# Routed two-layer mixture-of-experts kernel: guard terms moved into a table's margin, a minimum in place of masks, and a search's and a balancing's first products at other places of the order

## The chip, the cores and the metric

One core of one Trainium2 chip runs the program. The time is device microseconds for one execution, as a median over several; the profile comes from one execution of its own. TensorE (PE in the profile, PEld for its weight loads), VectorE (DVE), ScalarE (ACT), GpSimd (POOL) and SyncE (SP) each work through their own list of instructions in the order in which it was written, and wait for each other by semaphores.

## The reference

Attention over 4 x 8 heads of 576 positions gives 2304 tokens of 512 numbers. Two expert layers follow, each with 8 experts and two weight matrices per expert.

```python
# first layer: each token to one expert, in the order of the logits, 288 tokens per expert at most
cap = N // E
order = np.argsort(-flat)
for idx in order:
    tok, e = (int(idx) // E, int(idx) % E)
    if assigned[tok] >= 0 or counts[e] >= cap:
        continue
    assigned[tok] = e
    counts[e] += 1
# h = relu(x[mask] @ w1[e]); out[mask] = h @ w2[e]

# second layer: all tokens through all experts, weighted by a balanced table
P = np.exp(logits - logits.max())
for _ in range(8):
    P /= P.sum(1, keepdims=True) + 1e-09
    P /= P.sum(0, keepdims=True) + 1e-09
    P *= N / E
out += P[:, e:e + 1] * (np.maximum(x @ w1[e], 0.0) @ w2[e])
```

## The kernel before

The order of every engine's work is written by hand: `interleave` (L700) runs a main generator, whose `yield`s say how many nanoseconds of TensorE work were just issued, and a side generator, whose `yield`s say how much of that work shall go by before its next part is issued. A smaller number puts the side's next part earlier into every engine's list.

The program has these parts. The attention goes first. `stage1` then runs the first layer, expert by expert, with the routing beside it. One `Router.phase` (L530) finds one expert's tokens. It searches a threshold over the bits of the logits in six counts (`STEPS`): VectorE compares the 18 x 128 logits with up to 64 candidates into a grid of zeros and ones `G` (`above`, L504, in two halves of 9 columns); TensorE sums the grid with 18 products (L576, into the bank `r`); VectorE compares the sums with the places left (`ok`, L585); TensorE multiplies once more (L588); VectorE takes the maximum (`cur`, L590), from it the next candidates `x`, and the next `G`. After the last count the chosen tokens are marked in `ze`, TensorE adds them up by a matrix of ones and a triangular one, `tri` (L618, L619), and VectorE makes each token's place in its expert's list of it: a running sum `pos` (L621), masked by `zv` (chosen and not beyond 288, L624 and L625), and the two halves of `pos` added (`r`, L627). From the places come the lists by which GpSimd gathers tokens and weights. `books` (L653) then takes the used tokens out of the next phase: `mask` is lowered by 100 where a token is used.

While phase `ph + 1` is searched, TensorE works on expert `ph`: `moe1` (first layer) and then `m2_l1`, `m2_l2` (the second layer's first expert, on a piece of 256 tokens). In `l1` (L907) a step is three products; ScalarE copies the upper half of each of the 8 results of a piece out of the bank (L912), VectorE the lower half (L913). These halves live in tiles that the profile calls `w1h` and `w1l` (`xt` and `xg` in the last two pieces). Beside this, gathered weights of the next expert are split into halves piece by piece: ScalarE the upper (L847), VectorE the lower one (`w1l<-raw`, L838). The parts come to VectorE in the order in which they were issued.

After the eight phases, `last` (L1410) runs the second layer's first expert on the last two pieces, with `direct(1)`, which makes sums and halves of the next expert's weights (L1028 to L1048), and `sinkhorn` as the side. `sinkhorn` (L1289) takes the maximum of the table `P` (128 x 18 x 8) over each partition (L1302), has TensorE transpose it (L1305), takes the maximum of that and scales it (L1306, L1307), spreads it by a product (L1309), and after the exponential (L1311) does eight rounds: sum over each row's 8 numbers, guard 1e-9, reciprocal, product; then a column sum by TensorE (L1322) and VectorE (L1323), guard, reciprocal, product. What is left of it runs beside the first block of `stage2` (`s_l1`, L1176), in which TensorE waits for additions of VectorE (L1147). `stage2` is the long part: seven experts over three blocks each, with a seven-product scheme.

Of the kernel before, what the change touches and what calls it, by code (L numbers as in the profile page):

```python
# [11 lines left out]
F32 = mybir.dt.float32  # L12
# [9 lines left out]
CAP = N // E  # L22
# [357 lines left out]
STEPS = [6, 5, 5, 5, 5, 6]  # L380
COUNT = 0x4B000000


# [23 lines left out]
def route_tables():  # L407
    p = np.arange(128)
    f = {}
    f["tri"] = -(p[:, None] > p[None, :]).astype(np.float32)  # L410
    c = np.arange(NC)
# [21 lines left out]
class Router:  # L433
# [96 lines left out]
    def phase(self, ph):  # L530
# [10 lines left out]
        if not last:  # L541
# [10 lines left out]
            for n, bits in enumerate(STEPS):  # L552
# [17 lines left out]
                for s in [slice(self.cut, NC)] if first else halves:  # L570
                    self.above(G, m, c, s)
                yield 2900 if n else 4000 if ph < 2 else 2500
                w = NC - 128 // T
# [46 lines left out]
        pos = wk.tile([128, 2 * NC], F32, name="pos")  # L620
        V.tensor_tensor_scan(out=pos, data0=self.one_f, data1=p[:, :2 * NC], initial=0.0, op0=OP.mult, op1=OP.add)  # L621
        zv = wk.tile([128, 2 * NC], F32, name="zv")
        V.tensor_add(pos, pos, p[:, 64:64 + 2 * NC])
        V.scalar_tensor_tensor(zv, pos, CAP + 0.5, ze, op0=OP.is_le, op1=OP.mult)  # L624
        V.tensor_mul(pos, pos, zv)  # L625
        r = wk.tile([128, NC], F32, name="r")
        V.tensor_add(r, pos[:, :NC], pos[:, NC:])  # L627
        g = wk.tile([128, NC], F32, name="g")
# [24 lines left out]
        def books():  # L653
            V.scalar_tensor_tensor(GA, bc(m), cur, A, op0=OP.is_gt, op1=OP.mult)
            V.tensor_scalar(ng, code, wx, -1e30, op0=OP.is_equal, op1=OP.mult)
            V.tensor_sub(self.left, self.left, wx)
            V.tensor_scalar(up, m, cur, -100.0, op0=OP.is_gt, op1=OP.mult)
            V.tensor_add(self.mask, self.mask, up)
            V.scalar_tensor_tensor(self.mask, zv[:, NC:], -100.0, self.mask, op0=OP.mult, op1=OP.add)
            V.tensor_add(Lm, Lm, be(ng))  # L660
# [57 lines left out]
class Moe:  # L718
# [547 lines left out]
    def load_gate2(self):  # L1266
        nc, sm = self.nc, self.sm
        g = sm.tile([128, KT, E], F32, name="g2f")
        self.g2 = sm.tile([128, KT, 2, E], F16, name="g2")
        self.P = sm.tile([128, NT, E], F32, name="P")  # L1270
        nc.sync.dma_start(g, self.wg2.rearrange("(k p) e -> p k e", p=128))
        nc.scalar.activation(self.g2[:, :, 0], g, AF.Copy, scale=SG)
        nc.vector.scalar_tensor_tensor(self.g2[:, :, 1], g, SG, self.g2[:, :, 0], op0=OP.mult, op1=OP.subtract)
# [15 lines left out]
    def sinkhorn(self):  # L1289
# [12 lines left out]
        V.tensor_reduce(mx, P, axis=AX.XY, op=OP.max)  # L1302
        yield 4200
        q = self.r.psum()
        nc.tensor.transpose(q[:1, :128], mx, self.idf)  # L1305
        V.tensor_reduce(m1, q[:1, :128], axis=AX.X, op=OP.max)  # L1306
        V.tensor_scalar(m1, m1, -1.0 / (SX2 * SG), None, op0=OP.mult)  # L1307
        yield 3000
        nc.tensor.matmul(q[:, 128:129], one_f[:1, :], m1, start=True, stop=True, skip_group_check=True)  # L1309
# [5 lines left out]
        for it in range(8):  # L1315
            V.tensor_reduce(rs, P, axis=AX.X, op=OP.add)
            V.tensor_scalar(rs, rs, 1e-9, None, op0=OP.add)
            V.reciprocal(rs, rs)
            V.tensor_mul(P, P, rs.unsqueeze(2).to_broadcast(full))
            yield 6000  # L1320
            q = self.r.psum()
            nc.tensor.matmul(q[:, :NT * E], mean, P.rearrange("p t e -> p (t e)"), start=True, stop=True)  # L1322
            V.tensor_reduce(cs, q[:, :NT * E].rearrange("p (t e) -> p e t", e=E), axis=AX.X, op=OP.add)  # L1323
            V.tensor_scalar(cs, cs, 1e-9 / CAP, None, op0=OP.add)
            V.reciprocal(cs, cs)
            V.tensor_mul(P, P, cs.unsqueeze(1).to_broadcast(full))
# [183 lines left out]
```

## Time and profile before

| | |
|---|---|
| median of 3 runs | 1766.63 us (1766.28 to 1768.82) |
| profiled execution | 1749.94 us, span 1748.2 us |
| TensorE busy | 1709.2 us (98% of the span), 14326 products |
| VectorE busy | 1341.8 us (77%), 2572 instructions |
| ScalarE busy | 845.9 us (48%) |
| GpSimd busy | 233.9 us (13%) |
| granted TensorE clock, mean | 0.989 |
| chain that ended last | PE 70%, issue 10%, DVE 8%, ACT 2%, POOL 1% |

Busy TensorE counts overlapping products, so a wait of a few tenths of a microsecond does not show in the share; it shows in the timeline, as idle time in brackets behind a row, with the instruction that ended it. The attention fills the first 110 us, phase 0 runs alone to about 139 us, the other phases to about 444 us, the last pieces to 582 us, and stage two from there.

### The profile page before, as it was taken

The numbers are of one execution on the slowest core, as the hardware profiler recorded it, in microseconds if no ns is written. First come the engines' busy times: TensorE is split into PE (matmuls) and PEld (weight loads), VectorE is DVE, ScalarE is ACT, GpSimd is POOL, SyncE is SP. The second block draws the span as 40 slices with busy tenths as digits, with TensorE's granted clock in tenths as the row PEclk, the third lists the DMA queues.
The fourth block names the chain that finished last, engine by engine and source line by source line (L and its number), as shares of the span: only waits on it lengthen the run. The fifth ranks groups of instructions, "written<-read, shape, count | busy, mean of one in ns | idle before, by whom it ended". The sixth has DMA issues, their size and how long they took to land.

```text
span 1748.2 us, 34876 instructions
## 1 busy us (share of the span) xinstructions
PE 1709.2 (98%) x14326; PEld 1280.5 (73%) x14326; DVE 1341.8 (77%) x2572; ACT 845.9 (48%) x1544; POOL 233.9 (13%) x293
## 2 busy tenths in 40 slices
PE   8988999999999899999999999999999999999998
PEld 7955677777777577777777777777777777777777
DVE  6977777777648788878887887888788878886656
ACT  6933443334444455644445543565445544454433
POOL 1323333223410000000000000000000000000111
PEclk9978999999999999999999999999999999999999
DMA  8923444332733244343435235432444334433020
GB/s 316 292 60 111 124 125 132 96 98 76 213 99 102 76 163 154 137 156 115 175 127 209 86 140 208 157 130 89 201 160 158 122 130 156 165 138 148 37 100 37
DMA packets 107568, 241.19 MB, mean 138 GB/s; under 512 B 46384, under 2 KB 72496, under 8 KB 100496
## 3 DMA queue, kind: packets, MB, share of 16 engines
q1 hardware_dynamic: 86768, 151.64, 25.1%
q0 software_dynamic: 20384, 87.05, 14.2%
q8 instruction: 112, 1.84, 0.4%
q14 instruction: 48, 0.39, 0.1%
q10 hardware_dynamic: 256, 0.28, 0.1%
HBM read 173.64 MB, written 61.73 MB: 135 GB/s over the span
## 4 chain that ended last, share of the span: by engine, by line
PE 70%; issue 10%; DVE 8%; ACT 2%; POOL 1%; DMA 0%; POOLq 0%; ACTq 0%; DVEq 0%
PE mm L1176 27%; PE mm L1214 25%; PE mm L907 8%; PE mm L992 5%; PE mm L948 3%; DVE hl L1133 1%; PE r L576 1%; POOL out_dram L1228 1%; DVE w2l L966 1%; DVE G L640 1%; ACT raw L1045 0%; DVE G L504 0%; DVE x2l L953 0%; PE mm L922 0%; DVE w1l L1048 0%
## 5 line engine op out<-in xcount | busy, mean ns | idle before, releaser
L1176 PE MATMUL mm<-xb,w1h 128*128 128x384 f16 x2352 | 573.3, 326 | 3.2 <-DVE mm L1147 2.9
L1214 PE MATMUL mm<-w2h,hh 128*128 128x256 f16 x1764 | 480.8, 273 | 0.4
L1214 PE MATMUL mm<-w2h,hl 128*128 128x256 f16 x1764 | 480.8, 273 | 0.0
L1214 PE MATMUL mm<-w2l,hh 128*128 128x256 f16 x1764 | 480.8, 273 | 0.0
L1176 PE MATMUL mm<-xb,w1l 128*128 128x384 f16 x1176 | 383.3, 326 | 0.0
L1214 PEld LDWEIGHTS <-hh 128*128 128x128 f16 x3528 | 345.2, 98 | 43.2 <-issue 1.0
L1176 PEld LDWEIGHTS <-w1h 128*128 128x128 f16 x2352 | 230.0, 98 | 156.6 <-issue 8.5
L1214 PEld LDWEIGHTS <-hl 128*128 128x128 f16 x1764 | 172.6, 98 | 19.9
L1133 DVE TENSOR_TENSOR hl<-r,hh 128x1536 f16<-128x1536 f32 x84 | 147.5, 1756 | 41.3 <-ACT hh L1132 41.3
L1176 PEld LDWEIGHTS <-w1l 128*128 128x128 f16 x1176 | 115.0, 98 | 76.1
L1128 ACT ACTIVATE r<-mm 128x384 f32<-128x384 f32 x252 | 119.1, 481 | 100.8 <-PE mm L1176 100.8
L1094 POOL DMA_DIRECT2D ws<-raw x48 | 26.1, 543 | 930.1 <-ACT raw L1045 532.2
L1132 ACT ACTIVATE hh<-r 128x1536 f16<-128x1536 f32 x84 | 124.6, 1483 | 43.6 <-DVE r L1157 41.6
L1139 ACT ACTIVATE mm<-mm 128x384 f32<-128x384 f32 x84 | 40.3, 480 | 175.3 <-PE mm L1176 175.3
L1133 DVE TENSOR_TENSOR hl<-S,hh 128x1152 f16<-128x1152 f32 x84 | 113.5, 1351 | 0.0
L1224 DVE SCALAR_TENSOR_TENSOR acc<-t,P,acc 128x512 f32<-128x512 f32 x126 | 94.7, 752 | 4.5
L1132 ACT ACTIVATE hh<-S 128x1152 f16<-128x1152 f32 x84 | 96.4, 1147 | 1.0 <-DVE S L1161 1.0
L907 PE MATMUL mm<-xt,w1h 128*128 128x288 f16 x512 | 96.8, 289 | 0.0
L1045 ACT ACTIVATE raw<-raw 128x1024 f16<-128x1024 f32 x48 | 50.6, 1055 | 87.6 <-DVE raw L1029 45.9
L912 ACT ACTIVATE w1h<-mm 128x288 f16<-128x288 f32 (+1 forms) x120 | 46.4, 396 | 89.3 <-PE mm L907 89.3
L913 DVE SCALAR_TENSOR_TENSOR w1l<-mm,w1h 128x288 f16<-128x288 f32 (+1 forms) x120 | 50.3, 436 | 47.7 <-ACT w1h L912 47.6
L868 POOL DMA_INDIRECT raw<-in_w2a_dram,widx x64 | 72.1, 1127 | 54.2 <-issue 18.9
(265 smaller groups left out, 2920.9 us busy)
## 6 DMA issues: line engine op xcount, KB each, us to landing
xb<-xw SPq DMA_DIRECT2D x30, 1344.0 KB, 5.9
ws<-raw POOLq DMA_DIRECT2D x48, 448.0 KB, 3.5
ws<-r POOLq DMA_DIRECT2D x48, 448.0 KB, 3.5
raw<-in_w2b_dram SPq DMA_DIRECT2D x32, 512.0 KB, 4.2
raw<-in_w1b_dram SPq DMA_DIRECT2D x56, 256.0 KB, 8.6
w1h<-ws SPq DMA_DIRECT2D x6, 1792.0 KB
w1l<-ws SPq DMA_DIRECT2D x6, 1792.0 KB
w2h<-ws SPq DMA_DIRECT2D x6, 1792.0 KB, 7.5
```

Source lines behind the costliest of these rows:

```text
L868: self.nc.gpsimd.indirect_dma_start(out=r[:, i, :], out_offset=None, in_=rows[lay], in_offset=bass.IndirectOffsetOnAxis(ap=widx[:, c:c + 1 ...
L907: nc.tensor.matmul(p, a[:, k, 128 * f:128 * (f + 1)], rhs(k, b), start=(done[f] == 1 and i == 0), stop=(done[f] == KT and i == 2), skip_gr ...
L913: nc.vector.scalar_tensor_tensor(h[1][:, f, :n], p, 0.0, h[0][:, f, :n], op0=OP.max, op1=OP.subtract)
L948: nc.tensor.matmul(p, a[:, f, c], b[:, f, :CAP], start=(f == 0 and i == 0), stop=(f == FT - 1 and i == 2))
L992: nc.tensor.matmul(p, a[:, f, c], b[:, f, :], start=(f == 0 and n == 0), stop=(f == FT - 1 and n == 2))
L1045: self.nc.scalar.activation(hi[:, k], x, AF.Copy, scale=sw)
L1128: nc.scalar.activation(o, p, AF.Relu, scale=SH)
L1132: yield nc.scalar.activation(hq[0][:, i, k], x, AF.Copy)
L1133: yield V.tensor_sub(hq[1][:, i, k], x, hq[0][:, i, k])
L1176: nc.tensor.matmul(p, w[u][:, 2 * j + i // 2, k, 128 * (i % 2):128 * (i % 2 + 1)], x[:, v, r, j], start=(q in (1, 5) and j == 0 and n == 0 ...
L1214: nc.tensor.matmul(p, h[u][:, i, a, 128 * t:128 * (t + 1)], w[v][:, i, b, :], start=(q in (1, 7) and i == 0 and j == 0), stop=(q in (2, 3) ...
L1224: V.scalar_tensor_tensor(self.acc[:, r, :], x, self.P[:, r, e:e + 1], self.acc[:, r, :], op0=OP.mult, op1=OP.add)
```

## The change

Three things are done. The places are made without a mask: the running sum begins at 1000 instead of 0, and the diagonal of `tri` takes 1000 off again for a marked token, so an unmarked one stays beyond every list; the two halves are joined by their minimum. `zv` and its product go away, and `books` gets a comparison and an addition in place of one masked addition. The table `P` gets a column of 1e-9 and a row of 1e-9/128, which the sums take in, so the two additions of the guard in each of the eight rounds go away; the column sum's product has 152 columns instead of 144. And four `yield`s change: the first count of phases 3 and later comes after 3300 instead of 2500, the second after 2150 instead of 2900; the balancing's first two products come after 2000 and 1800 instead of 4200 and 3000.

```diff
@@ -379,6 +379,7 @@
 NC = NT
 STEPS = [6, 5, 5, 5, 5, 6]
 COUNT = 0x4B000000
+FAR = 1000.0
 
 
 def step_constants():
@@ -407,7 +408,7 @@
 def route_tables():
     p = np.arange(128)
     f = {}
-    f["tri"] = -(p[:, None] > p[None, :]).astype(np.float32)
+    f["tri"] = -(p[:, None] > p[None, :]).astype(np.float32) - FAR * np.eye(128, dtype=np.float32)
     c = np.arange(NC)
     base = 128 * c
     val = np.zeros((128, NC, 2), np.float32)
@@ -569,7 +570,7 @@
                 p = self.psum()
                 for s in [slice(self.cut, NC)] if first else halves:
                     self.above(G, m, c, s)
-                yield 2900 if n else 4000 if ph < 2 else 2500
+                yield (2150 if n == 1 and ph > 2 else 2900) if n else (4000, 4000, 2500, 3300)[min(ph, 3)]
                 w = NC - 128 // T
                 for i in (*range(w), *range(w + 1, NC), w):
                     g = self.wide(G, i)
@@ -618,13 +619,10 @@
         nc.tensor.matmul(p[:, :2 * NC], self.ones, ze, start=True, stop=True)
         nc.tensor.matmul(p[:, 64:64 + 2 * NC], self.tri, ze, start=True, stop=True, skip_group_check=True)
         pos = wk.tile([128, 2 * NC], F32, name="pos")
-        V.tensor_tensor_scan(out=pos, data0=self.one_f, data1=p[:, :2 * NC], initial=0.0, op0=OP.mult, op1=OP.add)
-        zv = wk.tile([128, 2 * NC], F32, name="zv")
+        V.tensor_tensor_scan(out=pos, data0=self.one_f, data1=p[:, :2 * NC], initial=FAR, op0=OP.mult, op1=OP.add)
         V.tensor_add(pos, pos, p[:, 64:64 + 2 * NC])
-        V.scalar_tensor_tensor(zv, pos, CAP + 0.5, ze, op0=OP.is_le, op1=OP.mult)
-        V.tensor_mul(pos, pos, zv)
         r = wk.tile([128, NC], F32, name="r")
-        V.tensor_add(r, pos[:, :NC], pos[:, NC:])
+        V.tensor_tensor(r, pos[:, :NC], pos[:, NC:], op=OP.min)
         g = wk.tile([128, NC], F32, name="g")
         V.tensor_scalar(g, r, QB + 0.5, None, op0=OP.is_ge)
         V.scalar_tensor_tensor(g, r, 2 * QB + 0.5, g, op0=OP.is_ge, op1=OP.add)
@@ -656,7 +654,8 @@
             V.tensor_sub(self.left, self.left, wx)
             V.tensor_scalar(up, m, cur, -100.0, op0=OP.is_gt, op1=OP.mult)
             V.tensor_add(self.mask, self.mask, up)
-            V.scalar_tensor_tensor(self.mask, zv[:, NC:], -100.0, self.mask, op0=OP.mult, op1=OP.add)
+            V.tensor_scalar(up, pos[:, NC:], CAP + 0.5, -100.0, op0=OP.is_le, op1=OP.mult)
+            V.tensor_add(self.mask, self.mask, up)
             V.tensor_add(Lm, Lm, be(ng))
 
         if not last:
@@ -1267,7 +1266,10 @@
         nc, sm = self.nc, self.sm
         g = sm.tile([128, KT, E], F32, name="g2f")
         self.g2 = sm.tile([128, KT, 2, E], F16, name="g2")
-        self.P = sm.tile([128, NT, E], F32, name="P")
+        self.Pe = sm.tile([128, NT + 1, E + 1], F32, name="P")
+        self.P = self.Pe[:, :NT, :E]
+        nc.vector.memset(self.Pe[:, :, E:], 1e-9)
+        nc.vector.memset(self.Pe[:, NT:, :E], 1e-9 / 128)
         nc.sync.dma_start(g, self.wg2.rearrange("(k p) e -> p k e", p=128))
         nc.scalar.activation(self.g2[:, :, 0], g, AF.Copy, scale=SG)
         nc.vector.scalar_tensor_tensor(self.g2[:, :, 1], g, SG, self.g2[:, :, 0], op0=OP.mult, op1=OP.subtract)
@@ -1300,12 +1302,12 @@
             yield wait
             self.gate2(j)
         V.tensor_reduce(mx, P, axis=AX.XY, op=OP.max)
-        yield 4200
+        yield 2000
         q = self.r.psum()
         nc.tensor.transpose(q[:1, :128], mx, self.idf)
         V.tensor_reduce(m1, q[:1, :128], axis=AX.X, op=OP.max)
         V.tensor_scalar(m1, m1, -1.0 / (SX2 * SG), None, op0=OP.mult)
-        yield 3000
+        yield 1800
         nc.tensor.matmul(q[:, 128:129], one_f[:1, :], m1, start=True, stop=True, skip_group_check=True)
         V.tensor_copy(mx, q[:, 128:129])
         nc.scalar.activation(P, P, AF.Exp, bias=mx, scale=1.0 / (SX2 * SG))
@@ -1313,15 +1315,14 @@
         rs = sm.tile([128, NT], F32, name="rs")
         cs = sm.tile([128, E], F32, name="cs")
         for it in range(8):
-            V.tensor_reduce(rs, P, axis=AX.X, op=OP.add)
-            V.tensor_scalar(rs, rs, 1e-9, None, op0=OP.add)
+            V.tensor_reduce(rs, self.Pe[:, :NT], axis=AX.X, op=OP.add)
             V.reciprocal(rs, rs)
             V.tensor_mul(P, P, rs.unsqueeze(2).to_broadcast(full))
             yield 6000
             q = self.r.psum()
-            nc.tensor.matmul(q[:, :NT * E], mean, P.rearrange("p t e -> p (t e)"), start=True, stop=True)
-            V.tensor_reduce(cs, q[:, :NT * E].rearrange("p (t e) -> p e t", e=E), axis=AX.X, op=OP.add)
-            V.tensor_scalar(cs, cs, 1e-9 / CAP, None, op0=OP.add)
+            q = q[:, :(NT + 1) * E].rearrange("p (t e) -> p t e", e=E)
+            nc.tensor.matmul(q, mean, self.Pe[:, :, :E], start=True, stop=True)
+            V.tensor_reduce(cs, q.rearrange("p t e -> p e t"), axis=AX.X, op=OP.add)
             V.reciprocal(cs, cs)
             V.tensor_mul(P, P, cs.unsqueeze(1).to_broadcast(full))
         V.tensor_scalar(P, P, 1.0 / (SX2 * SW1 * SW2 * SH), None, op0=OP.mult)
```

VectorE, search phases 3 to 6, from the first grid of a phase to the second one. `w1l<-mm` is the lower half of a result, `w1l<-raw` that of a weight piece. Before, and as changed:

```order
L504 TENSOR_TENSOR G<-m,thr 128x576 x2
L913 SCALAR_TENSOR_TENSOR w1l<-mm,w1h 128x256 x3
L585 TENSOR_TENSOR ok<-r,rem 64x8
L838 SCALAR_TENSOR_TENSOR w1l<-raw,w1h 128x1024
L913 SCALAR_TENSOR_TENSOR w1l<-mm,w1h 128x256
L590 TENSOR_REDUCE cur<-r 128x1
L594 SCALAR_TENSOR_TENSOR pen,first<-index,cur,thr 128x64
L558 TENSOR_TENSOR x<-thr,first 128x32
L504 TENSOR_TENSOR G<-m,x 128x288 x2
```

```order
L505 TENSOR_TENSOR G<-m,thr 128x576 x2
L912 SCALAR_TENSOR_TENSOR w1l<-mm,w1h 128x256 x3
L837 SCALAR_TENSOR_TENSOR w1l<-raw,w1h 128x1024
L586 TENSOR_TENSOR ok<-r,rem 64x8
L912 SCALAR_TENSOR_TENSOR w1l<-mm,w1h 128x256 x2
L837 SCALAR_TENSOR_TENSOR w1l<-raw,w1h 128x1024
L591 TENSOR_REDUCE cur<-r 128x1
L595 SCALAR_TENSOR_TENSOR pen,first<-index,cur,thr 128x64
L559 TENSOR_TENSOR x<-thr,first 128x32
L505 TENSOR_TENSOR G<-m,x 128x288 x2
```

The first count now stands two steps of three products later in TensorE's list (23 steps of the piece ahead of it instead of 21). Two weight pieces have come ahead of `ok` and of `cur`; before, one stood between these two and one behind the second grid. The second count's products stand where they stood, nine products into `m2_l2`.

VectorE, the piece before the last, from the table's maximum to the scaled one and the first sum of rows. `xg<-mm` is the lower half of a result there, `raw<-raw` a sum of the next expert's weights. Before (where the first sum of rows comes six rows further on), and as changed:

```order
L1302 TENSOR_REDUCE mx<-P 128x1
L1048 SCALAR_TENSOR_TENSOR w1l<-raw,w1h 128x768
L913 SCALAR_TENSOR_TENSOR xg<-mm,xt 128x256
L1028 TENSOR_TENSOR raw<-raw 128x256
L1029 TENSOR_TENSOR raw<-raw 128x256
L1030 TENSOR_TENSOR raw<-raw 128x256
L1031 TENSOR_TENSOR raw<-raw 128x256
L913 SCALAR_TENSOR_TENSOR xg<-mm,xt 128x256 x2
L1306 TENSOR_REDUCE m_8012<-r 1x1
L1307 TENSOR_SCALAR m_8012<-m_8012 1x1
```

```order
L1304 TENSOR_REDUCE mx<-P 128x1
L1047 SCALAR_TENSOR_TENSOR w1l<-raw,w1h 128x768
L912 SCALAR_TENSOR_TENSOR xg<-mm,xt 128x256
L1027 TENSOR_TENSOR raw<-raw 128x256
L1028 TENSOR_TENSOR raw<-raw 128x256
L1029 TENSOR_TENSOR raw<-raw 128x256
L1030 TENSOR_TENSOR raw<-raw 128x256
L1308 TENSOR_REDUCE m_7997<-r 1x1
L1309 TENSOR_SCALAR m_7997<-m_7997 1x1
L912 SCALAR_TENSOR_TENSOR xg<-mm,xt 128x256 x2
L1312 COPY mx<-r 128x1
L1318 TENSOR_REDUCE rs<-P 128x18
```

The scaled maximum (`m`) now stands ahead of two result halves and not behind them. In TensorE's list the transposition has moved from behind 39 of that piece's products after the last gate to behind 21, and the product that spreads the scaled maximum from 24 products behind the transposition to 18. Five of the eight column sums now lie ahead of stage two, where four did; on ScalarE the exponential has moved ahead of two result halves.

VectorE, first block of stage two, from the third addition (L1158, now L1157) to the second of the additions that TensorE waits for (`mm<-mm`, L1147, now L1146), second chain. Before, and as changed:

```order
L1158 TENSOR_TENSOR S<-S,r 128x384
L1323 TENSOR_REDUCE cs<-r 128x8
L1324 TENSOR_SCALAR cs<-cs 128x8
L1325 RECIPROCAL cs<-cs 128x8
L1326 TENSOR_TENSOR P<-P,cs 128x144
L1316 TENSOR_REDUCE rs<-P 128x18
L1317 TENSOR_SCALAR rs<-rs 128x18
L1318 RECIPROCAL rs<-rs 128x18
L1319 TENSOR_TENSOR P<-P,rs 128x144
L1147 TENSOR_TENSOR mm<-mm,t_8675 128x384
```

```order
L1157 TENSOR_TENSOR S<-S,r 128x384
L1325 TENSOR_REDUCE cs<-r 128x8
L1326 RECIPROCAL cs<-cs 128x8
L1327 TENSOR_TENSOR P<-P,cs 128x18x8
L1328 TENSOR_SCALAR P<-P 128x18x8
L1146 TENSOR_TENSOR mm<-mm,t_8655 128x384
```

The chain there was a column step and a row step with a guard in each; it is now the last column step and the final scaling. Ahead of the following `mm<-mm` a short chain stood, and none stands there now.

## Rows read from the trace of the kernel before

**Rows 1.** Windows: stretch, busy time (instructions) of PE, PEld, DVE, ACT, POOL; clock, DMA share, GB/s.

```profile
776.00:1568.00 792.00, 791.73 (x6072) 593.70 (x6070) 645.82 (x998) 395.72 (x625) 42.81 (x79) 1.00 0.40 149
```

**Rows 2.** Timeline, PE, phase 4: start, length, engine, line, operation, count, [idle before <- releaser].

```profile
291.90 0.27 PE L907 MATMUL mm<-x2l,w0h 128*128 128x256 f16 x1
...
292.65 0.36 PE L576 MATMUL r<-A,G 128*128 128x8 f16 x8 [0.48 <-DVE G L504]
293.32 0.59 PE L576 MATMUL r<-A,G 128*128 128x8 f16 x10 [0.31 <-DVE G L504]
293.77 0.27 PE L907 MATMUL mm<-x2h,w0h 128*128 128x256 f16 x1
...
299.52 0.77 PE L576 MATMUL r<-A,G 128*128 128x8 f16 x18
```

**Rows 3.** Timeline, DVE, end of phase 3 and phase 4.

```profile
278.61 0.20 DVE L624 SCALAR_TENSOR_TENSOR zv<-pos,ze 128x36 f32<-128x36 f32 x1
...
279.07 0.18 DVE L627 TENSOR_TENSOR r<-pos 128x18 f32<-128x18 f32 x1
...
286.14 0.18 DVE L659 SCALAR_TENSOR_TENSOR mask<-zv,mask 128x18 f32<-128x18 f32 x1
...
291.84 1.42 DVE L504 TENSOR_TENSOR G<-m,thr 128x576 f16<-128x576 f32 x2
...
294.25 1.21 DVE L838 SCALAR_TENSOR_TENSOR w1l<-raw,w1h 128x1024 f16<-128x1024 f32 x1
295.42 0.42 DVE L913 SCALAR_TENSOR_TENSOR w1l<-mm,w1h 128x256 f16<-128x256 f32 x1
296.37 0.17 DVE L590 TENSOR_REDUCE cur<-r 128x1 f32<-128x8 f32 x1 [0.52 <-PE r L588]
...
297.12 0.87 DVE L504 TENSOR_TENSOR G<-m,x 128x288 f16<-128x288 f32 x2
```

**Rows 4.** Chain that ended last, phase 1: start, length, engine, what.

```profile
175.19 0.21 DVE zv L624
```

**Rows 5.** Waits of PE in 583.7:613 (total, times, longest), then its timeline.

```profile
PE mm L1176 <- DVE mm L1147: 2.9, 3, 1.1
...
594.35 0.33 PE L1176 MATMUL mm<-xb,w1l 128*128 128x384 f16 x1
595.46 0.32 PE L1176 MATMUL mm<-xb,w1h 128*128 128x384 f16 x1 [0.79 <-DVE mm L1147]
```

**Rows 6.** Timeline, DVE, first block of stage two.

```profile
592.65 0.30 DVE L1323 TENSOR_REDUCE cs<-r 128x8 f32<-128x144 f32 x1
592.99 0.17 DVE L1324 TENSOR_SCALAR cs<-cs 128x8 f32<-128x8 f32 x1
593.19 0.20 DVE L1325 RECIPROCAL cs<-cs 128x8 f32<-128x8 f32 x1
...
594.85 0.56 DVE L1147 TENSOR_TENSOR mm<-mm,t 128x384 f32<-128x384 f32 x1
...
609.16 0.30 DVE L1323 TENSOR_REDUCE cs<-r 128x8 f32<-128x144 f32 x1
...
610.43 0.56 DVE L1147 TENSOR_TENSOR mm<-mm,t 128x384 f32<-128x384 f32 x1
```

**Rows 7.** Timeline, DVE and PE, the last two pieces ahead of stage two.

```profile
543.77 0.30 DVE L1302 TENSOR_REDUCE mx<-P 128x1 f32<-128x144 f32 x1
...
546.78 0.42 DVE L913 SCALAR_TENSOR_TENSOR xg<-mm,xt 128x256 f16<-128x256 f32 x1
...
545.11 0.27 PE L1305 MATMUL r<-idf,mx 128*1 128x128 f32 x1
...
549.08 0.38 PE L1309 MATMUL r<-m,one_p 1*128 1x1 f32 x2 [0.45 <-DVE m L1307]
...
576.40 0.39 PE L992 MATMUL mm<-w1h,xg 128*128 128x512 f16 x1 [1.59 <-DVE xg L913]
```

**Rows 8.** Timeline, ACT, phase 4.

```profile
301.42 1.06 ACT L847 ACTIVATE w2h<-raw 128x1024 f16<-128x1024 f32 x1 [2.25 <-DMA raw<-in_w2a_dram,widx]
```

## The prediction

> **What bounds the kernel now.** I read the windows first. In the long second stage TensorE is busy 791.73 of 792 us [rows 1], so nothing on another engine can shorten that part, and whatever is won or lost before it arrives whole at the end. The change touches only what lies ahead: the eight phases of the routing search, the last two pieces of the second layer with the balancing beside them, and the first block of stage two. There I looked for what TensorE waits for.
>
> In the search phases the reader is to see one wait per phase. In phase 4 TensorE has a slot free at 292.01 (its last product started at 291.90, and these products follow each other every 0.11 us), starts the first count's products at 292.65, stops again until 293.32 for the second half of the grid G, and is back at its own work at 293.77 [rows 2]. VectorE started that G at 291.84 [rows 3]; a first half reaches TensorE 0.81 later, the second 0.67 after it. The second count starts at 299.52 with no wait [rows 2], though its G was started at 297.12 [rows 3]. Phases 3 to 6 repeat this.
>
> In the first block of stage two TensorE waits three times, 2.9 us in all, for an addition (L1147) [rows 5]. The second read there is VectorE's own order: each of those additions stands behind a chain of balancing steps, the first from 592.65 to 594.85, a second of the same make, and a last one from 609.16 to 610.43 [rows 6]. By slots a wait is longer than recorded: the next product was due 0.16 us after 594.35, came at 595.46, so 0.95 was lost where 0.79 is shown [rows 5]. Three times 0.16 more makes 3.4 us.
>
> Between the two, TensorE waits 0.45 us at 549.08 for the balancing's scaled maximum and 1.59 at 576.40 for VectorE's low halves [rows 7].
>
> **The change, term by term.**
>
> *Place as a minimum.* Two steps go from VectorE's chain in each phase: from 278.61 to 279.07, 0.46 us [rows 3]. One comes back later: the mask update becomes a comparison and an addition, and both wait for the step before. I price the extra one by the 0.18 of the old update [rows 3] and a gap like the others between dependent steps, 0.26 in all. Net, the chain reaches the next phase's G 0.20 earlier. In phase 1 the removed steps stand on the chain of waits itself [rows 4], and phase 0, where nothing else runs, has the same order. So phases 1 and 2 gain 0.2 each: **0.4 us** (bounds 0, if the added steps cost as much as the two removed, and 0.9).
>
> *First count later, phases 3 to 6.* Two steps of three products, 6 x 0.109 = 0.65 us, now stand ahead of the first count. TensorE does them while G is being made, and with G 0.20 earlier the count ends 0.85 us earlier in TensorE's work. But the queue behind it changes too. The first weight piece's low half, 1.17 from one start to the next (294.25 to 295.42 [rows 3]), now stands ahead of `ok`, and the second piece, of the same size, ahead of `cur`. `ok` comes at about 295.2 against a slot for its product at 295.9, so that is covered. `cur` is not: the sixth result is split at about 296.2, the piece takes 1.17, `cur` starts at 297.4 instead of 296.37, and the second G, 0.75 behind it as now (296.37 to 297.12 [rows 3]), at 298.1. Its halves are ready at some 298.6 and 299.0 (half of the 0.87 of both [rows 3], and the hand-over). TensorE, 0.85 ahead, wants them at 299.52 - 0.85 = 298.67. So the second count, which waits for nothing now, waits about 0.2. Net 0.65 in each of four phases: **2.6 us**. Bounds: 0.2 each (the second count waits 0.65) and 0.95 each, so 0.8 to 3.8.
>
> *Guard in an extra row and column.* Of each full chain two steps go. One costs 0.20 (592.99 to 593.19 [rows 6]) and its twin as much: 0.42 with the gaps, on a chain of 2.20. The two new memsets stand in phase 0 behind a grid, while VectorE would wait for that grid's products; they cost nothing, and if that cover went, some 0.2 each. The table's rows become 9 numbers apart, which no row of this trace shows; I take no cost.
>
> [...]
>
> *Balancing moved forward.* The yields 4200, 3000 become 2000, 1800, and one whole round moves from the block to the time before it. The order shows three chains in the block instead of four: the first ahead of its first addition, where VectorE waited for TensorE anyway, a full one ahead of the second addition, the last short one ahead of the third, none ahead of the fourth. So the first stall falls from 0.95 to 0.54. The second chain, 2.2, becomes the short one, 1.27 less 0.21; with the 0.41 already gained that leaves a stall under 0.1. The third stall has no chain in front, and the 1.27 [rows 6] exceed its whole stall. Of 3.4 us some 0.6 remain: **2.75 us** (bounds 2.0 and 3.4).
>
> *What the nearer first products cost.* In TensorE's order the transposition of the maxima stood behind 39 products after the last gate and now stands behind 21. Its slot moves from 545.11 [rows 7] to 543.15, but the maxima end at 543.77 + 0.30 [rows 7]: a new wait of 1.0. The scaled maximum then stands right behind four sums, at the place of the row at 546.78 [rows 7], ends 0.45 later, and its product, due at 546.2, waits 1.1 where now it waits 0.6 by slots. Against these 2.1 us stand that 0.6 and the wait at 576.40, 1.74 by slots: VectorE has as many chains ahead of it as before, each 0.42 shorter, and reaches it half a microsecond earlier, while TensorE comes 1.6 later, so it closes. **0.3 us** gained (bounds: 1.5 lost, if that wait stays whole, and 2.3 gained, if nothing new is waited for).
>
> **Sum.** 0.4 + 2.6 + 2.75 + 0.3 = 6.0 us. The profiled execution took 1749.94 us with a span of 1748.2; it becomes about 1743.9. The median of the runs shown, 1766.63, is 16.7 above it; I take the same microseconds from it: **1760.6 us**.
>
> **The rivals.**
>
> *The search gives it back.* Four times the second count waits as long as the first did, because `cur` now stands behind a weight piece. For: my own margin there is 0.05 us at the first half. Against: the piece's ScalarE half is done long before. Gain 0.4 + 2.75 + 0.3 = 3.45, 1763.2.
>
> *The balancing stays late.* The two new waits are paid and the wait at 576.40 remains, since VectorE now idles for each nearer product instead of filling the time. Gain 6.0 - 1.7 = 4.3, 1762.3.
>
> *The stalls of the block do not close.* Another of VectorE's steps, the splits of 1.75 and 1.35 us, turns out to hold the additions, and only the shorter chain counts: 0.4 instead of 2.75. Gain 3.7, 1762.9.
>
> *Slower: weight pieces that wait for their gather ahead of the count.* Two pieces per phase now stand in front of `ok` and `cur`. Did they wait for their gather as the second layer's pieces do (2.25 us at 301.42 [rows 8]), VectorE and with it the count would stand twice per phase: 4.5, less the 0.7 of slack at `ok` and the 0.65 gained, 3.2 in each of four phases, 13 us lost against 3.45 won: 1776.2. It decides if a gathered first-layer piece lands after TensorE has come to the count; the pieces' ScalarE halves show no wait of that kind now, so I give it little.
>
> **How the numbers follow.** A measurement of this kernel tells about 0.2%, 3.5 us, from no change. Forecast 0.60; the search gives back 0.15; balancing late 0.12; the block's stalls stay 0.08; slower 0.05. Forecast and the balancing case end beyond 3.5 us but for a few hundredths each; the first rival ends just inside, the third on the line. That is 0.74 faster, 0.20 same, 0.06 slower. The range takes in all but the slower case and the bounds of the terms taken together at their far ends: from 7.8 us gained (search 3.6, block 3.2, the rest 1.0) to 1.8 gained.
>
> **What would show it.** In the changed profile: TensorE's wait for the first G in phases 3 to 6 falls from 0.79 to about 0.2 and one of 0.1 to 0.2 appears before the second count; the phases' period falls by 0.65. At the balancing's transposition and scaled maximum there are waits near 1 us each, and the wait near 576 is gone. In the block one wait of about 0.4 is left of three. The forecast is wrong if the period does not fall, if waits for `ok` or `cur` of 0.5 or more appear, or if the long wait near the end of the second layer stays.

## The result, and the profile after

The changed kernel was slower: median 1775.96 us of 6 runs (1773.79 to 1778.6) against 1766.47 of the kernel before, ratio 1.0052 [1.0039, 1.0065]. The prediction was 1760.6, in a range from 1758.8 to 1764.8: wrong in sign. The profiled execution is one of those runs (1774.41 us, span 1772.6). The page of after, its first lines and the row of clocks:

```profile
span 1772.6 us, 34859 instructions
...
PE 1721.7 (97%) x14326; PEld 1285.7 (73%) x14326; DVE 1336.7 (75%) x2549; ACT 844.4 (48%) x1544; POOL 233.7 (13%) x293
...
PEclk9967999999999999999999999999999999999999
```

The same products, 23 instructions fewer on VectorE, and the span 24 us longer (by the medians it is 9.5; the profiled execution of before was far below its own median). The windows of after (stretch, busy time and instructions of PE, PEld, DVE, ACT, POOL, clock, DMA share, GB/s) show where not to look: stage two is as full as in [rows 1]. The search phases are not; TensorE makes 465 and 452 products in the first two of these stretches, where the kernel before makes 514 and 515 (the repeated run, below).

```profile
240.00:293.00 53.00, 50.13 (x465) 35.63 (x464) 35.13 (x100) 19.59 (x35) 16.07 (x15) 0.97 0.34 98
293.00:346.00 53.00, 49.40 (x452) 34.28 (x450) 33.72 (x104) 19.06 (x35) 12.73 (x13) 0.94 0.35 91
...
315.00:320.00 5.00, 3.78 (x26) 1.70 (x26) 2.83 (x8) 4.02 (x6) 0.00 (x0) 0.51 0.20 60
...
776.00:1568.00 792.00, 791.71 (x6018) 588.58 (x6017) 641.89 (x991) 396.94 (x631) 40.99 (x76) 1.00 0.39 148
```

TensorE's waits of after, 187 to 620 us (total, times, longest). "issue" is time in which the engine waits for nothing that the profile shows; the profile of before had none of it in this stretch.

```profile
PE r L577 <- issue: 8.4, 11, 1.2
PE mm L906 <- issue: 2.6, 7, 0.5
PE mm L921 <- issue: 1.9, 3, 0.9
PE r L577 <- DVE G L505: 1.4, 3, 0.7
PE r L1311 <- DVE m L1309: 0.9, 1, 0.9
PE r L1307 <- DVE mx L1304: 0.8, 1, 0.8
...
PE mm L1175 <- DVE mm L1146: 0.4, 1, 0.4
```

The forecast's own waits are there, at its sizes: maxima 0.8 (1.0 forecast), scaled maximum 0.9 (1.1), one wait of 0.4 left in the block, none at the end of the second layer (1.59 in [rows 7]), and of G's two waits [rows 2] only the second half's 0.31. What came on top is 13.7 us of "issue", of which four times 0.31 are that wait under another name. In the timeline of TensorE, phase 3, it sits inside the third count:

```profile
254.29 1.19 PE L921 MATMUL mm<-id,xg 96*128 96x96 f16 x24
...
255.97 0.33 PE L577 MATMUL r<-A,G 128*128 128x8 f16 x7
257.50 0.22 PE L577 MATMUL r<-A,G 128*128 128x8 f16 x3 [1.20 <-issue]
258.92 0.52 PE L577 MATMUL r<-A,G 128*128 128x8 f16 x8 [1.20 <-issue]
...
260.73 0.63 PE L991 MATMUL mm<-w1h 128*128 128x512 f16 x1
261.16 0.63 PE L991 MATMUL mm<-w1l,w1h 128*128 128x512 f16 x1
```

and the weight loads of the same time come one or two at a time, 0.71 us apart:

```profile
256.80 0.10 PEld L577 LDWEIGHTS <-G 128*128 128x128 f16 x1 [0.61 <-issue]
257.51 0.11 PEld L577 LDWEIGHTS <-G 128*128 128x128 f16 x2 [0.61 <-issue]
```

G is not what it waits for: VectorE made it from 255.13 to 255.96, and the count began at 255.97. From 260.7 us the products follow each other in 0.43 us instead of 0.215: the clock granted was half (0.50 from 260.5 to 263.5 us, and 0.51 from 315 to 320, behind the next phase's stall, in the windows above). The phases, 52.56 us apart before (from the first product of one first count to that of the next), are 52.87, 56.67, 58.90 and 55.12 apart.

### The profile page after: what moved, and what is told of

It is laid out like the page before. It is cut to its first block, busy times and chain, and to the rows that moved or that the text cites. A ratio compares the mean times of both kernels' runs of the same rounds, so it can differ in the third digit from the quotient of the medians.

```text
span 1772.6 us, 34859 instructions
## 1 busy us (share of the span) xinstructions
PE 1721.7 (97%) x14326; PEld 1285.7 (73%) x14326; DVE 1336.7 (75%) x2549; ACT 844.4 (48%) x1544; POOL 233.7 (13%) x293
## 4 chain that ended last, share of the span: by engine, by line
PE 78%; issue 11%; DVE 7%; ACT 2%; POOL 1%; DMA 1%; SPq 0%; POOLq 0%; DVEq 0%; ACTq 0%
PE mm L1175 27%; PE mm L1213 25%; PE mm L906 9%; PE mm L991 6%; PE mm L947 4%; PE r L577 2%; PE ps_v L228 1%; DVE hl L1132 1%; PE ps_s L181 1%; POOL out_dram L1227 1%; PE ps_p L207 1%; PE mm L921 1%; PE ps_s L174 1%; DVE G L505 1%; ACT raw L1044 0%
## 5 line engine op out<-in xcount | busy, mean ns | idle before, releaser
L906 PE MATMUL mm<-x2l,w0h 128*128 128x256 f16 x288 | 78.5, 272 | 1.6 <-issue 0.9
```

The costliest lines, as they stand in the source:

```text
L906: nc.tensor.matmul(p, a[:, k, 128 * f:128 * (f + 1)], rhs(k, b), start=(done[f] == 1 and i == 0), stop=(done[f] == KT and i == 2), skip_gr ...
```

## What the change set free: the gathers

GpSimd gathers the next expert's weights, for the second layer with eight instructions per phase. In the timeline of POOL, phase 3, the third gather of before (the run repeated beside the experiments) waited; that of after does not:

```profile
247.68 0.96 POOL L868 DMA_INDIRECT raw<-in_w2a_dram,widx  x1 [2.95 <-ACT w1h L912]
248.94 1.18 POOL L868 DMA_INDIRECT raw<-in_w2a_dram,widx  x1 [0.30 <-DVE G L504]
251.53 1.53 POOL L868 DMA_INDIRECT raw<-in_w2a_dram,widx  x1 [1.41 <-ACT w1h L847]
```

```profile
247.34 0.96 POOL L867 DMA_INDIRECT raw<-in_w2a_dram,widx  x1 [2.79 <-ACT w1h L911]
248.60 1.03 POOL L867 DMA_INDIRECT raw<-in_w2a_dram,widx  x1 [0.30 <-issue]
249.94 1.18 POOL L867 DMA_INDIRECT raw<-in_w2a_dram,widx  x1 [0.30 <-DVE G L505]
```

It needs a buffer (`raw`) that VectorE frees with the lower half of the second weight piece. Before, that step stood behind the second grid, at 249.56; the changed order has it ahead of `cur`, at 247.59 (timelines of DVE, the repeated run and after). The gather follows the end of that step by 0.75 there, as it does in the first profile. The row names ScalarE's half (L847), done 1.0 before; with VectorE's step put back alone (comparison 6 below) the gather follows that step by 0.76 again and ScalarE's last half by 1.7, so it is VectorE's that it waits for.

```profile
248.48 0.83 DVE L504 TENSOR_TENSOR G<-m,x 128x288 f16<-128x288 f32 x2
...
249.56 1.22 DVE L838 SCALAR_TENSOR_TENSOR w1l<-raw,w1h 128x1024 f16<-128x1024 f32 x1
```

```profile
247.59 1.22 DVE L837 SCALAR_TENSOR_TENSOR w1l<-raw,w1h 128x1024 f16<-128x1024 f32 x1
248.73 0.16 DVE L591 TENSOR_REDUCE cur<-r 128x1 f32<-128x8 f32 x1
```

So the transfers, which paused for 1.5 us, now run through. In the view of the transfers from 252 to 253 us (queue, kind: packets, MB, share of 16 engines) the repeated run of before has one packet of a gather (q0) and one of instructions (q8); after has 61 of a gather:

```profile
q8 instruction: 1, 0.02, 7.5%
q0 software_dynamic: 1, 0.00, 0.1%
```

```profile
q0 software_dynamic: 61, 0.22, 61.9%
```

From this came, behind the first four runs below, theory D: TensorE's instructions come over the same transfer engines, and under unbroken gathers they come late. Rival E: the gathers don't matter, it is the counts' new place among TensorE's instructions. The trace of before has 112 packets on q8 ("instruction" in the view above, a share of the same 16 engines), of 16384 bytes each, and from the start of one to that of the next TensorE begins 255 products and weight loads in the mean (191 to 327). So I take them for its instructions, in blocks of about 256: an estimate, from these packets and from 14326 products with as many weight loads. In the stretch of [rows 1] 47 of these packets move, and TensorE stands for 0.27 us in all; whether the waits here are waits for such a packet, no run shows.

The packets' own records do not bear out that the instructions come late. In phase 3 the last packet of q8 starts at 251.90, takes 1.34 us (1.19 for the one of the repeated run of before) and is in 3 us before TensorE stops at 256.3; the next one starts at 269.77. In phases 5 and 6 it is in 0.5 and 0.7 us before TensorE stops, and only in phase 4 does one run during a stall. So D makes two claims: that TensorE stands when the gathers run without a pause, which the runs below test, and that it then waits for instructions, which none of them shows; what the expectations call waits for instructions are the "issue" waits.

## The experiments

Six comparisons, each on one chip with runs of the kernel before beside it, gave:

| comparison, before (us) | kernel | us | ratio [95%] |
|---|---|---|---|
| 1: 1766.47 | changed (result) | 1775.96 | 1.0052 [1.0039, 1.0065] |
| 2: 1760.42 | before again | 1760.64 | 1.0002 [0.9989, 1.0015] |
| | search's yields alone | 1768.21 | 1.004 [1.0025, 1.0055] |
| | all but the search's yields | 1756.84 | 0.9979 [0.9964, 0.9993] |
| | places alone | 1760.47 | 1.0003 [0.9988, 1.0017] |
| 3: 1767.53 | changed + pause | 1764.68 | 0.9983 [0.9969, 0.9997] |
| | split earlier | 1771.73 | 1.0026 [1.0012, 1.004] |
| | first count alone | 1781.23 | 1.0082 [1.0053, 1.0111] |
| | second count alone | 1775.6 | 1.0052 [1.0036, 1.0067] |
| 4: 1751.73 | changed, second split later | 1743.39 | 0.9956 [0.9939, 0.9973] |
| | changed + half a pause | 1745.13 | 0.9963 [0.9946, 0.9979] |
| | guard alone | 1749.84 | 0.9986 [0.9975, 0.9998] |
| | nearer products alone | 1752.07 | 1.0002 [0.9991, 1.0012] |
| 5: 1751.92 | changed again | 1743.88 | 0.9955 [0.9942, 0.9969] |
| | second split later | 1744.06 | 0.9955 [0.9941, 0.9968] |
| | all but the search's yields | 1746.02 | 0.9974 [0.9964, 0.9984] |
| 6: 1760.17 | second split later | 1758.9 | 0.9993 [0.9981, 1.0006] |
| | changed, third time | 1766.3 | 1.0033 [1.002, 1.0045] |

**Which part loses.** Four kernels: before unchanged; only the search's yields; everything but them; only the lines of the places.

```diff
-                yield 2900 if n else 4000 if ph < 2 else 2500
+                yield (2150 if n == 1 and ph > 2 else 2900) if n else (4000, 4000, 2500, 3300)[min(ph, 3)]
```

> The kernel before, unchanged. Its profiled execution took 1749.94 us, its timed ones 1766.5 (16.5 more), and the changed kernel's profile shows TensorE waiting for its own instructions ('issue', 13.7 us between 187 and 520 us, in pieces of 0.4 to 1.2 us, all while the routing's gathers run) and a granted clock at half speed behind several of these waits; the earlier profile of before has no such wait. Theory A (waits for instructions are usual, and the first profile of before was an exception): this profile has a span near 1764 and issue waits of 5 to 15 us between 187 and 520 us. Theory B (the issue waits are the change's own): no issue wait on TensorE there, and the 16 us lie elsewhere, ahead of 187 us (the half clock lasting longer there) or in stage two.

> Only the two yields of the search are changed (first count 3300 instead of 2500 from phase 3 on, second 2150 instead of 2900). My forecast had 2.6 us of gain for it. Theory A (the moved count puts TensorE's next block of instructions under the gathers): this alone is slower than before by 6 to 12 us, with issue waits in phases 3 to 6 as in the changed kernel. Theory C (the loss comes with the places as a minimum or with the balancing): 0 to 4 us faster than before, issue waits no larger than in before.

> The changed kernel with the search's two yields as before. Theory A: faster than before by 2 to 5 us (what I forecast for the other three parts, 3.4), that is 6 to 12 us faster than the changed kernel. Theory C: as slow as the changed kernel within 4 us.

> Only the places as a minimum (no mask zv). Forecast: 0.4 us faster (0 to 0.9), so no difference that can be told. Theory C for this part: the chain is 0.2 shorter per phase, so the gathers come earlier against TensorE's blocks of instructions, and issue waits change: 5 to 10 us slower.

Before again: span 1761.8, so the first profile (1749.94) was not typical of these runs. Yet it is theory B that holds in the phases: they are 52.57, 53.30, 52.58 and 52.56 apart, and the "issue" time at the counts is that of waits for G, 0.31 to 0.48 each. Its 13.6 us more lie ahead of phase 2 (3.9), in the phases (0.8), between the search and stage two (6.8, among it 3.35 for gathered tokens at 473.51) and behind. The search's yields alone lose 7.8 us, 6.1 of "issue" at the counts, phases of 55.24, 57.49 and 53.64; all the rest wins 3.6 where 3.4 was forecast. Places alone: nothing.

**Is it the pause?** In the changed kernel, fill the buffer on GpSimd ahead of the third gather; and the reverse, the buffer freed earlier in the kernel before, without moving a count. Beside them each yield alone.

```diff
+            if lay and k == per and 2 <= ph <= 5:
+                self.nc.gpsimd.memset(r, 0.0)
```

```diff
-            while len(back) > (n not in (KT - 1, len(todo) - 1)):
+            early = (1,) if key[0] == "a" and 2 <= key[1] <= 5 else ()
+            while len(back) > (n not in (*early, KT - 1, len(todo) - 1)):
```

> The changed kernel, with one added step on GpSimd: in the four phases ahead of the second layer's second weight piece (its third gather) GpSimd first fills that piece's buffer with zeros, so that the gathers pause by about a microsecond, as they do in the kernel before, where that gather waits for VectorE to free the buffer. No count and no weight piece is moved back. Theory D (the changed order frees the buffer about 2 us earlier, the gathers run on without a pause, and TensorE's own instructions, which come over the same transfer engines, are late): the waits for instructions in phases 3 to 6 are gone, and it is faster than before by 4 to 7 us (the 3.6 of the kernel without the search's edits, and up to 2.6 for the counts), 11 to 14 faster than the changed kernel. Theory E (the gathers do not matter; it is the counts' or products' new place against TensorE's blocks of instructions): no faster than the changed kernel, that is 6 to 12 us slower than before.

> The kernel before, in which only the lower half of the second first-layer weight piece is made earlier on VectorE in the four phases (right behind the first piece's, ahead of cur instead of behind the second grid). No count moves. Theory D: the buffer is free earlier, the gathers do not pause, and waits for instructions of 2 to 5 us per phase appear: 5 to 12 us slower than before. Theory E: within 2 us of before (cur has some 0.7 us of room).

```diff
-                yield 2900 if n else 4000 if ph < 2 else 2500
+                yield 2900 if n else (4000, 4000, 2500, 3300)[min(ph, 3)]
```

> The kernel before with only the first count's yield changed (3300 instead of 2500 from phase 3). It puts the second weight piece ahead of cur, as the whole change does. Theory D: slower than before by 5 to 12 us, with the waits for instructions. Theory E: no prediction of its own beyond the counts' places; between 3 us faster and 12 slower.

```diff
-                yield 2900 if n else 4000 if ph < 2 else 2500
+                yield (2150 if n == 1 and ph > 2 else 2900) if n else 4000 if ph < 2 else 2500
```

> The kernel before with only the second count's yield changed (2150 instead of 2900 from phase 3). The second weight piece stays behind the second grid. Theory D: the pause of the gathers stays, no waits for instructions in phases 3 to 6, within 3 us of before. Theory E: like the full search edits, 5 to 10 us slower, if this yield is the one that matters.

The fill takes 0.97 us. With it the lists of TensorE and VectorE are those of the changed kernel, row for row, and the stalls inside the counts are gone in all four phases. By E they would have stayed, since the counts stand where the change put them. One gap is left: the changed kernel itself did not run in this comparison, and that it would stall on this chip is taken from the first count alone, below; comparison 6 closes it. The pause won 2.9 us and not 4 to 7, since another wait came. Its waits:

```profile
PE r L589 <- DVE ok L586: 4.2, 4, 1.1
PE mm L908 <- issue: 2.3, 3, 1.1
```

Freeing the buffer earlier lost 4.2 us (5 to 12 expected): "issue" waits of 0.22, 0.35, 0.35 and 0.41 appeared in three phases. D's sign, but only a part of the loss lies in those waits. The first count alone lost most: phases 53.35, 59.50, 58.71 and 54.76 apart, with issue waits at 255.92 and 257.35, one of 2.09 for G and one of 3.37 for `ok`. The second count alone is a miss for D: 8 us lost, hardly any of it in "issue" waits in the phases, by waits of 0.4 to 1.8 for G and of 1.4 and 0.8 for `ok`. Its pause is in place in phases 3 and 4 only (1.41 and 1.10 us ahead of the third gather) and gone in 5 and 6 (0.30), though no weight piece was moved. The two late `ok` lie in phases 3 and 4, with the pause in place.

**The order alone.** The changed kernel with the second piece's lower half put back behind the second grid; and half the fill.

```diff
-            while len(back) > (n not in (KT - 1, len(todo) - 1)):
+            hold = key[0] == "a" and 2 <= key[1] <= 5 and n == 2
+            while len(back) > (2 if hold else n not in (KT - 1, len(todo) - 1)):
```

> The changed kernel with nothing added: only the lower half of the second weight piece goes back behind the second grid (three pieces in a row there), in the four phases. The counts stay where the change put them. Theory D (the unbroken gathers make TensorE's instructions late): GpSimd's third gather again waits for the buffer, the gathers pause, and TensorE's waits for instructions in the four phases are gone; but three pieces of 1.17 now stand ahead of the second count's comparison, which comes at about 254.4 on the changed kernel's clock where its product is due at 253.5, so a wait of up to 1 us per phase appears: between 5 us faster than before and no change. Theory E (the counts' new place): as slow as the changed kernel, 6 to 12 us slower than before.

```diff
-                self.nc.gpsimd.memset(r, 0.0)
+                self.nc.gpsimd.memset(r[:, :1], 0.0)
```

> As the kernel with the pause by a fill on GpSimd, but only half the buffer is filled, so the third gather is held back by about 0.5 us instead of 1. Theory D: if it is the break in the traffic that lets TensorE's instructions through, half of it may or may not do: either no such waits as with the full pause (then about 3 us faster than before, or up to 6 if the late comparison goes too), or waits in some phases (then between before and the changed kernel).

Both won the 6.0 us that the forecast had for the change and more, 8.3 and 6.6, without an issue wait in the phases, which are 51.66 and 51.83 apart from phase 3 on. But in this comparison the kernel before took 1751.73, so the changed kernel had to be run beside it.

**The balancing in two parts** (the lines of the table's margin alone; the two yields alone).

```diff
-        yield 4200
+        yield 2000
...
-        yield 3000
+        yield 1800
```

> The kernel before with only the guard in the table's margin; balancing's yields as before. By my terms each full chain is 0.42 shorter: in the first block of stage two the waits of 0.79, 1.02 and 1.08 fall to about 0.4, 0.6 and 0.9, and the wait of 1.59 for xg at the end of the second layer goes or nearly so: 1 to 2.7 us from the gates to the end of the block. Rival: the waits in the block are ended by other steps of VectorE and stay.

> The kernel before with only balancing's two yields changed. By my terms two new waits of about 0.8 to 1.1 appear (maxima, scaled maximum) against the old 0.45, the wait of 1.59 at the end of the second layer closes since one more round lies ahead of it only if VectorE has the time (else it stays), and in the block the third wait goes and the second shrinks by 0.9: 0.5 to 2.5 us in all. Rival: the wait at the end of the second layer stays whole and the sum is about zero.

From the gates' last wait (0.61 for xg, 541.83 in the first profile) to the wait for `t` behind the block, 629.99 there, the time falls from 88.2 us to 86.0 with the guard alone, to 86.8 with the yields alone, to 85.45 with both. The guard's waits in the block are 0.38, 0.62 and 0.86; the yields' are 0.79 and no other; the wait at the end of the second layer falls to 0.27 and 0.22.

**On one chip.**

> The changed kernel, unchanged, beside the next two on one chip. The kernel before has had medians from 1751.7 to 1767.5 in the comparisons so far, and the kernel with the second piece put back was measured where before was fastest. If theory D's loss belongs to the order and not to one chip: 5 to 12 us slower than before here too, with waits for instructions in phases 3 to 6 and GpSimd's third gather issued without a wait. If not: within 3 us of before, or faster.

> The changed kernel with the second weight piece's lower half behind the second grid, again. Theory D: no waits for instructions in phases 3 to 6, a period of 51.7 in phases 4 to 6 against 52.6 of before; 4 to 10 us faster than before and 10 to 20 faster than the changed kernel.

> The changed kernel with the search's two yields as before, again: 2 to 5 us faster than before, and behind the kernel with the second piece put back by the counts' gain, 0.65 to 0.9 in each of four phases, 2.6 to 3.6 us.

> The changed kernel with the second weight piece's lower half behind the second grid, a third time, beside the changed kernel. Where before takes over 1758 us here (the comparisons in which TensorE waited for instructions): theory D has this 3 to 12 us faster than before, without waits for instructions in phases 3 to 6. Where before takes about 1752: 8 us faster, like the changed kernel.

> The changed kernel a third time. Where before takes over 1758 us: 5 to 12 us slower than before, with waits for instructions of 2 to 4 us in each of the phases 3 to 6. Where before takes about 1752: 8 us faster.

In comparison 5 the changed kernel, the same program, is 8 us *faster* than before (D had 5 to 12 slower), with phases of 52.33, 51.84, 51.84 and 51.84. The gathers run through there too (the third is issued 0.30 behind the second), and TensorE does not stand. Its waits from 187 to 620 us:

```profile
PE r L1311 <- DVE m L1309: 0.9, 1, 0.9
PE r L1307 <- DVE mx L1304: 0.8, 1, 0.8
PE r L577 <- DVE G L505: 0.7, 1, 0.7
PE mm L906 <- DVE xg L912: 0.6, 1, 0.6
PE mm L1175 <- DVE mm L1146: 0.4, 1, 0.4
PE r L577 <- issue: 0.3, 1, 0.3
```

In comparison 6 (before 1760.17) it loses 6.1 us again, with 10.3 us of issue waits (windows' clocks 0.94, 0.94 and 0.97). With the piece put back, where only VectorE's order differs, it is level with before (3 to 12 us faster expected): no issue wait in the counts but one of 0.3 at G, and the late `ok` of the pause kernel again, 4.5 us in four:

```profile
PE r L589 <- DVE ok L586: 4.5, 4, 1.3
PE mm L907 <- ACT xt L923: 2.4, 1, 2.4
PE mm L907 <- issue: 2.0, 2, 1.1
```

**What comes late.** The trace also records the engines' signals to each other (semaphore updates). In after, 59 of TensorE's 385 signals from 110 to 620 us are recorded at least 0.2 us behind the end of their product, 58 of them with packets of a gather beside them; in before repeated 46 of 395, in the first profile 0 of 399, in the changed kernel of comparison 5 0 of 401. In phase 3 the three groups of transpositions (L921) end at 254.80, 255.14 and 255.48; their signals come at 258.93 to 259.12, and only then does ScalarE take the first result (timelines of ACT, after and comparison 5, where that group ends at 250.14 and the signal comes at 250.16):

```profile
258.96 2.21 ACT L922 ACTIVATE xt<-mm 128x768 f16<-128x768 f16 x3 [5.83 <-remote]
```

```profile
250.18 2.22 ACT L922 ACTIVATE xt<-mm 128x768 f16<-128x768 f16 x3 [1.61 <-PE mm L921]
```

In all four phases the last long "issue" wait ends as such held-up signals come: TensorE goes on at 258.92, 315.81, 374.54 and 429.68, the signals come at 258.93, 315.81, 374.53 and 429.69. The late `ok` is the same thing: in the pause kernel the third count's sums end at 257.11, their signal comes at 260.51, and VectorE starts `ok` at 260.53. That TensorE stands because its signals back up fits these times better than D's late instructions, but no run tests it.

So in these runs the long stalls in the phases came with both: gathers without a pause, which the order decides, and a chip, or an occasion, on which TensorE stands under them (comparisons 1, 2, 3 and 6). In comparison 5 the order made no difference (1743.88 us changed, 1744.06 with the piece put back). The version with the piece put back was never behind before: 8.3 and 7.9 us faster in two comparisons, level in one; on the chip that lost, it is 7.4 us ahead of the changed kernel.

## Why the prediction was wrong, step by step

**The step that failed** is "First count later", at "the queue behind it changes too". I saw that two weight pieces come ahead of `ok` and `cur`, priced them as delays of those two, and stopped. What the earlier piece releases I did not ask: it frees the buffer 2 us sooner, GpSimd's queue runs on, and on the chip on record TensorE stands while it does. Forecast 0.65 us gained per phase; on the chip on record 4.11, 6.34 and 2.56 lost (56.67, 58.90 and 55.12 against 52.56) in the three full periods from phase 3 on. My slower rival named weight pieces and gathers, but had VectorE waiting for a gather; that is not where it went, and that its 1776.2 is almost the 1775.96 measured is luck. Why TensorE stands while they run stays open; what the trace shows late there is its signals, by up to 4 us.

**A warning I passed over**: the profiled execution lay 16.7 us below the median, and I carried the difference over as a constant. It was an execution like those of comparisons 4 and 5. For that kind the sum holds: with the changed kernel of comparison 5 against [rows 2], the period falls by 0.72 (0.85 less a new 0.2 forecast, so 0.65; the second count takes 0.94 instead of 0.77), and the span by 6.1 (6.0 forecast); timed, 8.0 with the interval from 5.4 to 10.2. On the chip on record the sign stays wrong all the same.

**Places as a minimum**: 0.2 per phase were there once VectorE had no other wait (52.32 against 52.56 with the search's yields undone, comparison 5). In comparison 2, alone, the steps fell away and VectorE waited 0.4 at x2l (L952) in their place: periods of 52.82 to 52.85, nothing won. What VectorE waits for next I had not asked.

**The block and the last two pieces**: right. 2.75 and 0.3 forecast, 88.2 less 85.45, so 2.7 us, measured for both together; the new waits 0.83 and 0.92, the one left 0.39:

```profile
568.86 0.27 PE L1307 MATMUL r<-idf,mx 128*1 128x128 f32 x1 [0.83 <-DVE mx L1304]
572.01 0.38 PE L1311 MATMUL r<-m,one_p 1*128 1x1 f32 x2 [0.92 <-DVE m L1309]
...
619.83 0.48 PE L1175 MATMUL mm<-xb,w1h 128*128 128x384 f16 x2 [0.39 <-DVE mm L1146]
```

That the table's new rows, 9 numbers apart, cost nothing was assumed without a row that shows it. With the guard alone the step over 144 columns took 310 ns against 308 before, and the first wait of the block shrank by 0.4.

## What to carry to other kernels

When a step that frees a buffer moves forward, follow the buffer to the queue that waits for it, and ask what its transfers then run beside; here a fill of 0.97 us ahead of the third gather took the stalls out of the counts. And where a profiled execution is far off the median of its own runs, find out which of the two the change will meet before adding up tenths: the same program won 8 us in one comparison and lost 9.5 in another.

## What I had not expected of the hardware

In these phases TensorE stood in a straight program with its inputs complete: one or two instructions per 0.71 us, for 2 to 4 us, in or behind bursts of short products (24 of 43 ns, then 18 of 35 ns). Of the 6.34 us that phase 4 lost, 3.06 are recorded waits; the clock granted behind them, 0.51 from 315 to 320 us and 0.81 from 320 to 325, makes some 3.4 more, an estimate from these two windows. The profile's rows show these stalls only as "issue". That they go with unbroken gathers is shown by the cure, the fill of 0.97 us; the packets' times do not support that TensorE waits for instructions, and in each of the four phases the last long wait ends within 0.01 us of a late signal of its own.

One program differs by 15 us between comparisons (before: 1751.7 to 1767.5), and a change's sign with it; the transfers' own times hardly do (0.17 to 0.18 us per packet of a gather in both kinds). The late signals tell the two kinds apart: of some 400 by TensorE from 110 to 620 us, 0 to 3 are late in the first profile and in the profiles of comparisons 4 and 5, 46 to 64 in all the others, the kernel before among them. What makes a chip of one kind is open, and so is whether it is the chip at all: the five comparisons of the experiments ran on five chips, so chip and occasion are not told apart.

Where the pause was restored on a chip of the slower kind, VectorE's `ok` of the third count came 3.4 us or more after its sums in each of four phases; with the piece put back on the other kind it did not. The wait is for TensorE's signal of those sums, and it is this signal that is recorded late.
